# ReZero on one core: another cut of the load plan, with a multiply as the mark for the first store

## The chip, the cores and the metric

The kernel runs on one core of one Trainium2 chip. The metric is the device time of one execution in microseconds (us), the median of several runs. Before the change three runs gave 151.32, 151.74 and 152.62 us, so the time to beat is 151.74 us.

## The reference

Two arrays of bfloat16, `x` and `fx`, each of 512 x 32 x 640 elements, and one number `alpha`:

```
def reference(x, fx, alpha):
    return x + alpha * fx
```

Each array holds 20.97 MB. Both are read once and the output is written once, 62.92 MB in all, and the arithmetic on an element is one multiply and one add.

## The kernel before, in words

Each array is laid over the 128 partitions of the on-chip memory. A partition gets 81920 consecutive elements, which the kernel counts as 160 units of K = 512 elements (lines 12 and 13). One unit is 1 KiB on each partition, 128 KiB over all of them. Everything lives in one tile `t` of 160 + 47.5 units per partition (line 78): `x` has its place at units 0 to 160, is added to in place and stored from there. `fx` has no place of its own: it is put into units that `x` has not reached yet, or into the spare 47.5 units at the end.

The order of the work is written out by hand in `PLAN` (lines 27 to 56). The loop at lines 125 to 131 issues the steps in that order. A step's letter names its kind:

- `x a b` loads units a to b of `x` to their own place (line 98); `f a b p` loads units a to b of `fx` to place p (line 102). Both are issued on the queue of SyncE (SP).
- `a` loads `alpha` (line 106), spreads it over the partitions with one TensorE matmul (line 110) and copies it to the on-chip memory (line 112).
- `m a b` multiplies units a to b of `fx` by `alpha` in place, on VectorE (line 115); `c a b` adds them to `x`, on VectorE (line 118).
- `s a b` stores units a to b (line 121), on SP's queue too. Behind a bar stands a step that the store waits for although it needs none of its data ("begins late", line 131).

Waits for data and for places follow from overlapping ranges of `t`. A load that overwrites a place has to wait until the adds that read the old `fx` there are done. SP issues its steps strictly in order, so everything behind a waiting step waits as well; all loads and stores use one hardware queue that 16 DMA engines serve. VectorE takes its multiplies and adds in the order of the plan.

In the plan before, ten loads bring the data: `x` 0 to 8, 8 to 64, 64 to 96, 96 to 114, 114 to 155 and 155 to 160, and `fx` 0 to 64, 64 to 111.5, 111.5 to 137.5 and 137.5 to 160. The first five of them wait for nothing. `x` 96 to 114 overwrites `fx` 0 to 18, `x` 114 to 155 overwrites more of `fx` 18 to 64 (which lies at 96 to 160), and so on. The first store (units 0 to 64) is held back until the load of `fx` 137.5 to 160 has landed. The last load is `x` 155 to 160, with rows of 5 KiB. Three stores end the program: 0 to 64, 64 to 128 and 128 to 160. A last SP step (line 133) waits for all but the last store.

Of the kernel before, what the change touches and what calls it, by code (L numbers as in the profile page):

```python
# [1 line left out]

# [4 lines left out]

ALU = mybir.AluOpType
F32 = mybir.dt.float32

P = 128
K = 512
ROW = 160
SPARE = 47.5

LANES = 8

PLAN = """
x 0 8
a
x 8 64  # L30
f 0 64 96
x 64 96
f 64 111.5 160
m 0 18
c 0 18
x 96 114
m 18 64
c 18 64
x 114 155
m 64 88  # L40
c 64 88
f 111.5 137.5 158
m 88 111.5
c 88 111.5
f 137.5 160 184
m 111.5 113.5
c 111.5 113.5
x 155 160
s 0 64 | f 137.5 160 184
m 113.5 137.5  # L50
c 113.5 137.5
m 137.5 160
c 137.5 160
s 64 128
s 128 160
"""


@with_exitstack
def kernel(  # L60
    ctx: ExitStack,
    tc: tile.TileContext,
    x: bass.AP,
    fx: bass.AP,
    alpha: bass.AP,
    out: bass.AP,
):
    nc = tc.nc
    xv, fv, ov = (
        t.flatten_outer_dims().rearrange("(p n) d -> p (n d)", p=P) for t in (x, fx, out)  # L70
    )
    assert xv.shape[1] == ROW * K

    consts = ctx.enter_context(tc.tile_pool(name="consts", bufs=1))
    psum = ctx.enter_context(tc.tile_pool(name="psum", bufs=1, space=bass.MemoryType.PSUM))
    flat = ctx.enter_context(tc.tile_pool(name="flat", bufs=1))
    ctx.enter_context(tc.manual_schedule())
    t = flat.tile([P, int((ROW + SPARE) * K)], x.dtype, name="t")
    info = mybir.DependencyInfo(mybir.DependencyClass.Sync, mybir.DependencyReason.DATA)

    lanes = {}
    lies = []
    done = []

    def at(a, b):
        return t[:, int(a * K) : int(b * K)]

    def of(v, a, b):
        return v[:, int(a * K) : int(b * K)]

    def place(a, b):
        for c, d, p in reversed(lies):
            if c <= a and b <= d:
                return at(p + a - c, p + b - c)
        raise ValueError(f"fx {a} to {b} lies nowhere in one piece")

    def load_x(a, b):
        done.append(nc.sync.dma_start(out=at(a, b), in_=of(xv, a, b)))  # L98

    def load_f(a, b, p):  # L100
        lies.append((a, b, p))
        done.append(nc.sync.dma_start(out=at(p, p + b - a), in_=of(fv, a, b)))

    def load_alpha():
        a_n = consts.tile([LANES, 1], alpha.dtype, name="a_n")
        done.append(nc.sync.dma_start(out=a_n[:], in_=alpha[None, :].to_broadcast([LANES, 1])))  # L106
        ones = consts.tile([1, P], alpha.dtype, name="ones")
        nc.vector.memset(ones[:], 1.0)  # L108
        a_ps = psum.tile([P, 1], F32, name="a_ps")
        done.append(nc.tensor.matmul(a_ps[:], ones[:], a_n[0:1, :], start=True, stop=True))  # L110
        lanes["a"] = consts.tile([P, 1], F32, name="a_f")
        nc.vector.tensor_copy(out=lanes["a"][:], in_=a_ps[:])  # L112

    def multiply(a, b):
        done.append(nc.vector.tensor_scalar_mul(place(a, b), place(a, b), lanes["a"][:]))  # L115

    def add(a, b):
        done.append(nc.vector.tensor_add(at(a, b), at(a, b), place(a, b)))  # L118

    def store(a, b):  # L120
        done.append(nc.sync.dma_start(out=of(ov, a, b), in_=at(a, b)))

    does = {"x": load_x, "f": load_f, "a": load_alpha, "m": multiply, "c": add, "s": store}
    begun = {}
    for step in filter(None, PLAN.split("\n")):
        step, *later = step.split(" | ")
        what, *numbers = step.split()
        does[what](*map(float, numbers))
        begun[step] = done[-1]
        for other in later:  # L130
            tc.add_manual_dep(done[-1].ins, begun[other].ins.name, info, reason="begins late")

    rest = nc.sync.nop(nofuse=True)
    for i in done[:-1]:
        tc.add_manual_dep(rest.ins, i.ins.name, info, reason="all but the last store")


# [1 line left out]
_INS = ['x', 'fx', 'alpha']  # L139
_OUTS = [((512, 32, 640), 'bfloat16')]  # L140


# [23 lines left out]
```

## Time and profile before

| What | Value |
|---|---|
| median of 3 runs | 151.74 us (151.32 to 152.62) |
| time of the profiled execution | 151.5 us |
| its span, first to last instruction | 149.7 us |
| VectorE busy | 66.5 us, 44% |
| share of the 16 DMA engines' time | 97.9% |
| bytes moved | 62.92 MB, mean 420 GB/s |

The profiled execution took 151.5 us while its span is 149.7 us, so 1.8 us lie around the span. In the profile's rows DVE is VectorE, SPq is the sequencer that issues DMAs from SyncE, and a line such as L115 is a line of the kernel above. A DMA's time "to landing" counts from its issue until its last data has been confirmed, so it includes the time that it stands in the queue behind others. In the windows of the trace, a DMA packet (one row of a transfer) is counted whole where it begins, so the share of a short window can be far over 1.

### The profile page before, as it was taken

The page shows a single profiled execution, that of the slowest core. Times are in us where ns is not written, and L with a number is a line of the kernel's source. Part 1 is how long each engine was busy: PE and PEld are TensorE (multiplying, and loading weights), DVE is VectorE, ACT ScalarE, POOL GpSimd, SP SyncE. Part 2 cuts the span into 40 slices and gives each one's busy share as a digit, 9 for nine tenths or more (in the row PEclk, how much of TensorE's full clock was granted, in tenths as well). Part 3 has the DMA queues.
Part 4 walks back from the last instruction along what each step waited for, and adds up shares of the span by engine and source line. Part 5 has one row for each costly group of instructions (what it writes and reads, how often), then busy time and mean ns, then how long its engine had stood idle before and what let it go on. Part 6 is the DMA issues. An engine that isn't in the chain of part 4 may idle for free.

```text
span 149.7 us, 91 instructions
## 1 busy us (share of the span) xinstructions
PE 0.2 (0%) x1; PEld 0.1 (0%) x1; DVE 66.5 (44%) x16; POOL 0.2 (0%) x4
## 2 busy tenths in 40 slices
PE   0000000000000000000000000000000000000000
PEld 0000000000000000000000000000000000000000
DVE  0000000000079999999999944999990000000000
POOL 0000000000000000000000000000000000000000
DMA  5997996969999899979898989996997969696996
GB/s 173 598 429 306 490 525 280 560 280 560 403 429 420 357 520 494 429 323 500 359 527 370 427 377 414 456 480 280 560 508 333 560 280 560 280 560 280 420 420 280
DMA packets 1888, 62.92 MB, mean 420 GB/s; under 512 B 224, under 2 KB 224, under 8 KB 352
## 3 DMA queue, kind: packets, MB, share of 16 engines
q1 hardware_dynamic: 1888, 62.92, 97.9%
HBM read 41.94 MB, written 20.97 MB: 420 GB/s over the span
## 4 chain that ended last, share of the span: by engine, by line
DMA 36%; DVE 34%; issue 4%; SPq 1%; DVEq 0%
DMA t<-in_fx_dram 36%; DVE t L118 21%; DVE t L115 13%; SPq L98 0%; SPq L106 0%; DVEq L115 0%
## 5 line engine op out<-in xcount | busy, mean ns | idle before, releaser
L118 DVE TENSOR_TENSOR t<-t 128x12288 bf16<-128x12288 bf16 (+5 forms) x7 | 43.8, 6255 | 0.2
L115 DVE TENSOR_SCALAR t<-t,a_f 128x12288 bf16<-128x12288 bf16 (+5 forms) x7 | 22.8, 3264 | 40.0 <-DMA t<-in_fx_dram 40.0
L112 DVE COPY a_f<-a_ps 128x1 f32<-128x1 f32 x1 | 0.2, 158 | 4.6 <-PE a_ps L110 4.6
L108 DVE MEMSET ones<- 1x128 bf16 x1 | 0.2, 165 | 0.8 <-PEq L150 0.8
L110 PE MATMUL a_ps<-a_n,ones 1*128 1x1 bf16 x1 | 0.2, 158 | 5.4 <-DMA a_n<-in_alpha_dram 5.4
L150 POOL MEMSET const-uint8-127<- 128x1 uint8 x1 | 0.1, 102 | 0.0
L150 POOL MEMSET const-bfloat16-1.0<- 128x1 bf16 x1 | 0.1, 101 | 0.0
L110 PEld LDWEIGHTS <-ones 1*128 1x128 bf16 x1 | 0.1, 98 | 1.0 <-DVE ones L108 1.0
L150 POOL MEMSET const-float32-0.0<- 128x1 f32 x1 | 0.1, 98 | 0.2 <-issue 0.2
L150 POOL MEMSET const-float32-1.0<- 128x1 f32 x1 | 0.1, 98 | 0.0
## 6 DMA issues: line engine op xcount, KB each, us to landing
t<-in_x_dram SPq DMA_DIRECT2D x1, 7168.0 KB, 20.9
t<-in_fx_dram SPq DMA_DIRECT2D x1, 6080.0 KB, 63.0
t<-in_x_dram SPq DMA_DIRECT2D x1, 5248.0 KB, 15.6
t<-in_x_dram SPq DMA_DIRECT2D x1, 4096.0 KB, 49.1
out_dram<-t SPq DMA_DIRECT2D x1, 4096.0 KB, 36.7
t<-in_fx_dram SPq DMA_DIRECT2D x1, 3328.0 KB, 13.5
t<-in_fx_dram SPq DMA_DIRECT2D x1, 2880.0 KB
t<-in_x_dram SPq DMA_DIRECT2D x1, 2304.0 KB, 21.9
```

Source lines behind the costliest of these rows:

```text
L108: nc.vector.memset(ones[:], 1.0)
L110: done.append(nc.tensor.matmul(a_ps[:], ones[:], a_n[0:1, :], start=True, stop=True))
L112: nc.vector.tensor_copy(out=lanes["a"][:], in_=a_ps[:])
L115: done.append(nc.vector.tensor_scalar_mul(place(a, b), place(a, b), lanes["a"][:]))
L118: done.append(nc.vector.tensor_add(at(a, b), at(a, b), place(a, b)))
L150: nc = _bacc.Bacc("TRN2", target_bir_lowering=False, num_devices=1)
```

## The change

Only `PLAN` changes; the functions that carry out its steps stay as they are.

```diff
-x 0 8
+f 0 8 95
 a
-x 8 64
-f 0 64 96
-x 64 96
-f 64 111.5 160
-m 0 18
-c 0 18
-x 96 114
-m 18 64
-c 18 64
-x 114 155
-m 64 88
-c 64 88
-f 111.5 137.5 158
-m 88 111.5
-c 88 111.5
-f 137.5 160 184
-m 111.5 113.5
-c 111.5 113.5
-x 155 160
-s 0 64 | f 137.5 160 184
-m 113.5 137.5
-c 113.5 137.5
-m 137.5 160
-c 137.5 160
+f 8 65 103
+x 0 64
+x 64 95
+f 65 112.5 160
+m 0 8
+m 8 65
+c 0 8
+c 8 64
+c 64 65
+x 95 160
+m 65 95
+c 65 95
+f 112.5 142.5 160
+m 95 112.5
+c 95 112.5
+f 142.5 160 190
+m 112.5 134.5
+s 0 64 | m 112.5 134.5
+m 134.5 142.5
+c 112.5 142.5
+m 142.5 160
+c 142.5 160
 s 64 128
 s 128 160
```

There are eight loads in place of ten. `fx` comes first: units 0 to 8 and 8 to 65, laid at 95 to 160. Then come `x` 0 to 64 and 64 to 95 and `fx` 65 to 112.5, again five loads that wait for nothing. `x` 95 to 160 is one load with rows of 65 KiB; it waits for the add of unit 64 to 65. `fx` 112.5 to 142.5 is laid at 160 and waits for the add of 65 to 95; `fx` 142.5 to 160, the last load, is laid at 190 and waits for the add of 95 to 112.5. VectorE has 7 multiplies and 7 adds as before, in other pieces: the first two multiplies both stand ahead of the first add. The first store is held back until the multiply of 112.5 to 134.5 is done, and no longer by a load. The stores are the same three.

## The prediction

> **What bounds the kernel now.** I read the page first: its span, the busy engines and the DMA queue.
>
> ```profile
> span 149.7 us, 91 instructions
> PE 0.2 (0%) x1; PEld 0.1 (0%) x1; DVE 66.5 (44%) x16; POOL 0.2 (0%) x4
> DMA  5997996969999899979898989996997969696996
> q1 hardware_dynamic: 1888, 62.92, 97.9%
> ```
>
> The one queue fills 97.9% of the 16 DMA engines' time, VectorE 44% of its own. The change moves the same bytes, so only the queue's losses can be won: its start, its end, a gap, or a stretch that runs below its pace. To find them I followed the queue from landing to landing, with the SP rows of the timeline (issue), the issue table (time to landing), the chain (two waits for a load) and line 121 (the stores).
>
> ```profile
> 0.73 0.38 SPq L98 DMA_DIRECT2D t<-in_x_dram  x1
> 2.93 0.58 SPq L102 DMA_DIRECT2D t<-in_fx_dram  x1
> 49.59 19.05 SPq L98 DMA_DIRECT2D t<-in_x_dram  x2
> 68.31 0.33 SPq L98 DMA_DIRECT2D t<-in_x_dram  x1
> 78.24 10.05 SPq L102 DMA_DIRECT2D t<-in_fx_dram  x2
> 87.96 0.33 SPq L102 DMA_DIRECT2D t<-in_fx_dram  x1
> 93.04 0.33 SPq L98 DMA_DIRECT2D t<-in_x_dram  x1
> 99.10 0.35 SPq L121 DMA_DIRECT2D out_dram<-t  x1
> ...
> t<-in_fx_dram SPq DMA_DIRECT2D x1, 6080.0 KB, 63.0
> t<-in_x_dram SPq DMA_DIRECT2D x1, 5248.0 KB, 15.6
> t<-in_x_dram SPq DMA_DIRECT2D x1, 2304.0 KB, 21.9
> t<-in_x_dram SPq DMA_DIRECT2D x1, 1024.0 KB, 4.9
> t<-in_x_dram SPq DMA_DIRECT2D x1, 640.0 KB, 7.6
> ...
> 1.96 39.89 DMA t<-in_fx_dram
> 78.24 13.53 DMA t<-in_fx_dram
> ...
> DMA to landing us min/median/max: 20.9/36.4/36.7
> ...
> SPq L121 <- DMA t<-in_fx_dram: 5.7, 1, 5.7
> ```
>
> Issue plus time to landing gives: x 0 to 8 at 0.73 + 4.9 = 5.6; fx 0 to 64 at 1.96 + 39.89 = 41.85; fx 64 to 111.5 at 2.93 + 63.0 = 65.9; x 96 to 114 at 49.59 + 21.9 = 71.5; x 114 to 155 at 68.31 + 15.6 = 83.9; fx 111.5 to 137.5 at 78.24 + 13.53 = 91.77; fx 137.5 to 160 at 99.1 (the store waits 5.7 for it and is issued at 99.10); x 155 to 160 at 93.04 + 7.6 = 100.6; the last store, issued last with the longest time (its row comes below), at 112.28 + 36.7 = 149.0.
>
> **Pace by stage, in us per unit (128 KiB).** Units 8 to 64 of x and 0 to 64 of fx: (41.85 - 5.6) / 120 = 0.302. The next 79.5 units: (65.9 - 41.85) / 79.5 = 0.303. Then 5.6 / 18 = 0.31, 12.4 / 41 = 0.302, 7.9 / 26 = 0.303. Then fx 137.5 to 160: (99.1 - 91.77) / 22.5 = 0.326. Then 1.5 / 5 = 0.30. The three stores: (149.0 - 100.6) / 160 = 0.302. So the queue never stands still at its slowest engine, and one load runs below the pace: fx 137.5 to 160 takes 7.33 where 22.5 x 0.302 = 6.80, a loss of 0.5. Everything else together is some 0.25 over the pace. The reader should keep this ceiling: 5.6 + 472 x 0.302 = 148.1 for the last landing, against 149.0. About 0.9 us, 0.6%, is all that a perfect queue could win.
>
> Before the first store I also looked at short windows, since a landing shows the slowest engine only.
>
> ```profile
> 99.00:99.25 0.25, 0.00 (x0) 0.00 (x0) 0.25 (x1) 0.00 (x0) 1.00 0.98 410
> 99.25:99.50 0.25, 0.00 (x0) 0.00 (x0) 0.25 (x1) 0.00 (x0) 1.00 0.85 348
> 99.50:99.75 0.25, 0.00 (x0) 0.00 (x0) 0.25 (x1) 0.00 (x0) 1.00 0.26 102
> 99.75:100.00 0.25, 0.00 (x0) 0.00 (x0) 0.25 (x1) 0.00 (x0) 1.00 3.94 1675
> 0.00:1.70 1.70, 0.00 (x0) 0.10 (x1) 0.17 (x1) 0.20 (x4) 1.00 0.00 0
> ```
>
> The last columns are the DMA share and GB/s. The share sinks to 0.85 and 0.26 while the loads run out, and the store's first rows begin only after 99.75, some 0.65 to 0.9 behind its issue at 99.10. The first load of the program, issued at 0.73, begins no row before 1.70 either. So a transfer needs about 0.7 to 1.0 from issue to its first row, and the store was issued too late for the quick engines: they idle about 0.15 x 0.25 + 0.74 x 0.25 + 0.2 = 0.4 on the mean. The slowest engine is not among them, as the pace above shows: there the slow load hides the late store.
>
> **The change part by part.** The base is the profiled execution: span 149.7, time 151.5, so 1.8 around the span; the median of the runs shown is 151.74, 0.24 above it.
>
> First, *ten loads become eight.* What a load costs beside its bytes is read from the shortest one: x 155 to 160 landed 1.5 after its forerunner and its 5 units are 5 x 0.302 = 1.51 by the pace. With the rounding of the rows that is 0 to 0.1 a load, so two fewer give 0 to -0.2; I take -0.1. The Trainium skill, page "DMA: Bandwidth & Descriptors", section "Anatomy of one DMA", states a fixed cost of about 2.0 us for a DMA (fitted for the path issued from GpSimd); by that, paid in series, the two loads would be worth 4 us; the trace disagrees for a queue that is fed ahead, by the 1.5 of the shortest load.
>
> Second, *the order of loads.* Up to fx 65 to 112.5 the queue carries 8 + 57 + 64 + 31 + 47.5 = 207.5 units without a wait, as before (8 + 56 + 64 + 32 + 47.5). Cost nothing; alpha is again second in the queue. Later loads must be issued about 1.0 before the queue runs dry. For that I need VectorE's durations.
>
> ```profile
> L118 DVE TENSOR_TENSOR t<-t 128x23552 bf16<-128x23552 bf16 x1 | 12.4, 12426 | 0.0
> L118 DVE TENSOR_TENSOR t<-t 128x9216 bf16<-128x9216 bf16 x1 | 5.0, 4959 | 0.0
> L115 DVE TENSOR_SCALAR t<-t,a_f 128x23552 bf16<-128x23552 bf16 x1 | 6.3, 6349 | 0.0
> L115 DVE TENSOR_SCALAR t<-t,a_f 128x9216 bf16<-128x9216 bf16 x1 | 2.6, 2620 | 36.2 <-DMA t<-in_fx_dram 36.2
> 112.28 0.33 SPq L121 DMA_DIRECT2D out_dram<-t  x1
> ```
>
> From the two adds: (12426 - 4959) / 14336 = 0.521 ns an element, 0.267 us a unit, and 0.16 fixed. From the two multiplies: 0.260 ns, 0.133 us a unit, and 0.22 fixed. Now the new plan in time.
>
> - fx 0 to 8 lands at 5.6, fx 8 to 65 at 5.6 + 57 x 0.302 = 22.8; both multiplies are done by 22.8 + 7.8 = 30.6, under cover of the load of x 0 to 64, which lands at 42.2. Adds: 0 to 8 takes 2.3, 8 to 64 takes 15.1, 64 to 65 takes 0.43 (x 64 to 95 landed at 51.6), all done at 60.0. Then x 95 to 160 is issued. The queue holds fx 65 to 112.5 until that lands at 65.9: margin 5.9, less 1.0.
> - m 65 to 95: 4.2 from 65.9, to 70.1. c 65 to 95: 8.2, to 78.3. fx 112.5 to 142.5 is issued there; the queue holds x 95 to 160 until 65.9 + 65 x 0.302 = 85.5. Margin 7.2.
> - m 95 to 112.5 (2.6) runs meanwhile; c 95 to 112.5 waits for x until 85.5 and takes 4.8, to 90.4. fx 142.5 to 160 is issued there; the queue holds fx 112.5 to 142.5 until 94.6. Margin 4.2, less 1.0: the tightest of the three.
>
> SP waits in order, but behind each wait stand only later loads and stores that cannot go earlier. So the three waits cost nothing; if the cover of the last were gone, say VectorE 4 us late there, the queue would stand still for about 0.8.
>
> Third, *the row of 65 KiB.* The longest row in this trace is 64 KiB, so its price is not shown. If the row is moved in two pieces, 128 rows more, it costs what a load of the same 128 rows costs beside its bytes, 0 to 0.1. From below nothing is gained but those two loads already counted, since 64 KiB rows run at the common pace. From above: if a row is cut into 65 pieces of 1 KiB, there are 64 x 128 rows more; at 0 to 0.1 for 128 rows that is at most 6.4, and 3.2 at the middle. I take 0.05, nearest to the rows of 64 KiB. The Trainium skill, same page, section "Why a DMA increments its semaphore by 16 and not by 1", says that a contiguous row over 64 KiB is cut into equal pieces by software, and one without a fitting divisor falls into one piece per element; 33280 elements have the divisor 16640, so by that page two pieces; no run here shows it yet.
>
> Fourth, *no short last rows.* The last two loads, 22.5 and 5 units, took 7.33 + 1.5 = 8.83 where the pace gives 8.31. Of the new last loads one has 30 units, nearest to the 26 that ran at 0.303, and one 17.5 units, nearest to the 18 that ran at 0.31 (loss 0.1 to 0.15). Bounds: the loss of 0.5 vanishes, or it comes again in the new last load, since nothing in the trace says why it was slow. I take -0.4.
>
> Fifth, *the store's mark.* fx 112.5 to 142.5 lands at 94.6; m 112.5 to 134.5 takes 22 x 0.133 + 0.22 = 3.15, so the store is issued at about 97.8 and can begin its rows at 98.5 to 98.8. The last load lands at 94.6 + 17.5 x 0.302 + 0.1 = 100.0; its rows end earlier, on the quick engines at about 99.0 to 99.2 (before, they thinned out from 99.25 with the last landing at 100.6). So no engine waits for the store; 0.4 of mean idle goes. By itself that moves the end by 0, since the slowest engine did not wait; with the slow load gone, the store issued at 99.10 would have become the next limit and eaten up to half of the 0.4 of step four. Both go together; I count the store's mark as 0 to -0.2 beyond step four, and take -0.05. What is late next is nothing but the queue itself.
>
> The stores 64 to 128 and 128 to 160 are issued after c 112.5 to 142.5 (97.8 + 1.3 + 8.2 = 107.3) and c 142.5 to 160 (107.3 + 2.6 + 4.8 = 114.7), the last some 2.4 later than the 112.28 of before. The queue holds the first store until about 119: hidden.
>
> Sum: -0.1 + 0.05 - 0.4 - 0.05 = -0.5. Span 149.2, profiled time 151.0, against the median 151.74 - 0.5 = 151.24, so 151.2.
>
> **The rivals.**
>
> A, the forecast: no new wait, the queue at its pace, 151.2; with its bounds (losses of 0 to 0.9 in all) 150.8 to 151.7.
>
> B, the change wins nothing: the slow load was an accident of memory traffic and hits the new last load as well. For it speaks that no wait explains it (it was issued at 87.96, 3.8 before its forerunner landed); against it, that all other stages ran at 0.30 to 0.31. Then 151.7.
>
> C, the other side: the row of 65 KiB is cut fine and the load of x 95 to 160 itself becomes slow. Its landing carries everything behind it along: c 95 to 112.5, the last load, the stores. Price 3.2 (the middle above), so 151.24 + 3.2 = 154.4; it decides (slower by over 1%, 1.5 us) from about 2 us extra, an additional 0.03 us per unit. For it: no row over 64 KiB stands in this trace. Against it: rows of 5 to 64 KiB all run within 0.01 of the same pace but for the one load.
>
> D, each load pays its fixed cost in full, as in the page's rule above. Then two fewer would give 4 us, 147.7. The mechanism here would be a queue that drains between loads; the short load's 1.5 speaks against it almost alone.
>
> E, the last load is issued too late, because x 95 to 160 is one piece and its add begins only when all of it has landed. With 3.2 of net margin it needs a VectorE add of 8 in place of 4.8; then 0.1 to 1 us, up to 152.2.
>
> **How the numbers follow.** A difference of 1% (1.5 us) is about what a measurement of this kernel can tell from no change; the three runs before lie 1.3 apart. Chances: A 0.62, B 0.12, C 0.10, D 0.02, E 0.04, and 0.10 for what I do not see. Of A, 0.02 could fall below 150.2, since the ceiling of 0.9 and the spread of the runs together reach that far; of the unseen I give 0.04 to faster and 0.05 to slower by over 1%. Faster: 0.02 + 0.02 + 0.04 = 0.08. Slower: C's 0.10 + 0.05 = 0.15. The rest, 0.77, is within 1%. The range: from A's lower bound less the runs' spread below their median (150.8 - 0.4 = 150.4) to E's 152.2 plus as much, 152.6; it leaves out C, D and the far ends.
>
> **What would show it.** Right: the store's issue at 97.5 to 98.2; no window around 99 with a DMA share under 0.9 for half a us; x 95 to 160 landing at 85.2 to 86; SP's waits for VectorE ending at about 60, 78 and 90; the last landing at 148.3 to 148.7. Wrong: more packets than 8 x 128 + 3 x 128 + 128 rows and alpha's few would show a finely cut row (and a landing of x 95 to 160 past 87); a window without DMA at 65, 85 or 94 would show a late issue; fx 142.5 to 160 taking over 5.7 would show that the slow last load stays.

## The result and the profile after

The changed kernel takes 151.09 us, the median of 18 runs (150.95 to 151.29), against 151.75 us for the kernel before (18 runs, 151.32 to 152.62). The ratio is 0.9952 with a 95% interval of 0.9939 to 0.9965: a small gain of about half a per cent, within the 1% that the forecast counts as no change, and 0.1 us below the 151.2 that it named. The spread of the runs shrank as well, from 1.30 to 0.34 us.

The first lines of the changed kernel's page, then its issue table, the SP rows of its timeline and the pieces of its chain that end in a landing:

```profile
span 149.3 us, 84 instructions
PE 0.2 (0%) x1; PEld 0.1 (0%) x1; DVE 66.5 (45%) x16; POOL 0.2 (0%) x4
DMA  5969998969699999999999999899896969697993
DMA packets 1728, 62.92 MB, mean 421 GB/s; under 512 B 192, under 2 KB 192, under 8 KB 192
q1 hardware_dynamic: 1728, 62.92, 98.0%
...
t<-in_x_dram SPq DMA_DIRECT2D x1, 8320.0 KB, 25.8
t<-in_fx_dram SPq DMA_DIRECT2D x1, 7296.0 KB, 21.4
t<-in_fx_dram SPq DMA_DIRECT2D x1, 6080.0 KB, 63.0
out_dram<-t SPq DMA_DIRECT2D x1, 4096.0 KB, 33.7
t<-in_fx_dram SPq DMA_DIRECT2D x1, 2240.0 KB, 9.5
...
1.59 0.35 SPq L100 DMA_DIRECT2D t<-in_fx_dram  x1
3.09 0.51 SPq L100 DMA_DIRECT2D t<-in_fx_dram  x1
60.07 0.38 SPq L96 DMA_DIRECT2D t<-in_x_dram  x1
78.58 12.53 SPq L100 DMA_DIRECT2D t<-in_fx_dram  x2
98.15 17.05 SPq L119 DMA_DIRECT2D out_dram<-t  x3
...
1.98 40.34 DMA t<-in_x_dram
78.58 16.36 DMA t<-in_fx_dram
```

The profiled execution took 151.11 us, the span is 149.3. The landings, worked out as in the forecast: fx 8 to 65 at 1.59 + 21.4 = 23.0, x 0 to 64 at 42.32, fx 65 to 112.5 at 3.09 + 63.0 = 66.1, x 95 to 160 at 60.07 + 25.8 = 85.9, fx 112.5 to 142.5 at 94.94, and fx 142.5 to 160, issued at 78.58 + 12.53 - 0.33 = 90.8, at 100.3. (The 0.33 is the time of one issue; the row holds two.) So the last load took 5.4 for its 17.5 units, 0.306 a unit: no load runs clearly below the pace any more. The last store was issued at 98.15 + 17.05 - 0.35 = 114.9 and landed 33.7 later, at 148.6, where it was 149.0 before.

The windows around the first store, with the DMA share in the last but one column:

```profile
98.00:99.00 1.00, 0.00 (x0) 0.00 (x0) 1.00 (x2) 0.00 (x0) 1.00 1.17 502
99.00:99.25 0.25, 0.00 (x0) 0.00 (x0) 0.25 (x1) 0.00 (x0) 1.00 0.67 287
99.25:99.50 0.25, 0.00 (x0) 0.00 (x0) 0.21 (x2) 0.00 (x0) 1.00 2.44 1049
99.50:99.75 0.25, 0.00 (x0) 0.00 (x0) 0.25 (x1) 0.00 (x0) 1.00 5.47 2359
99.75:100.00 0.25, 0.00 (x0) 0.00 (x0) 0.25 (x1) 0.00 (x0) 1.00 1.82 786
100.00:100.25 0.25, 0.00 (x0) 0.00 (x0) 0.25 (x1) 0.00 (x0) 1.00 0.00 0
```

A row of 64 KiB occupies one of 16 engines for about 2.42 us, so one that begins in a window of 0.25 us adds 2.42 / 0.25 / 16 = 0.6 to its share. The reader can count engines: 2.44, 5.47 and 1.82 are 4, 9 and 3 engines that begin the store, each as its own loads run out, and by 100.0 all 16 have begun. Before the change there was a hole (0.26 in the window from 99.50), and one row more of the same view shows three engines that began after 100.25:

```profile
100.25:100.50 0.25, 0.00 (x0) 0.00 (x0) 0.25 (x1) 0.00 (x0) 1.00 1.82 786
```

### The profile page after: what moved, and what is told of

The parts are those of the page before. It is cut to its first block, busy times and chain, and to the rows that moved or that the text cites. A ratio compares the mean times of both kernels' runs of the same rounds, so it can differ in the third digit from the quotient of the medians.

```text
span 149.3 us, 84 instructions
## 1 busy us (share of the span) xinstructions
PE 0.2 (0%) x1; PEld 0.1 (0%) x1; DVE 66.5 (45%) x16; POOL 0.2 (0%) x4
## 2 busy tenths in 40 slices
DMA packets 1728, 62.92 MB, mean 421 GB/s; under 512 B 192, under 2 KB 192, under 8 KB 192
## 3 DMA queue, kind: packets, MB, share of 16 engines
q1 hardware_dynamic: 1728, 62.92, 98.0%
## 4 chain that ended last, share of the span: by engine, by line
DMA 38%; DVE 33%; another core or an unknown queue 4%; SPq 1%; issue 0%; DVEq 0%
DMA t<-in_x_dram 27%; DVE t L116 26%; DMA t<-in_fx_dram 11%; DVE t L113 7%; SPq L100 0%; SPq L104 0%; DVEq L116 0%
## 5 line engine op out<-in xcount | busy, mean ns | idle before, releaser
L116 DVE TENSOR_TENSOR t<-t 128x15360 bf16<-128x15360 bf16 (+4 forms) x7 | 43.6, 6252 | 16.6 <-DMA t<-in_x_dram 16.5
L113 DVE TENSOR_SCALAR t<-t,a_f 128x4096 bf16<-128x4096 bf16 (+4 forms) x7 | 22.8, 3265 | 25.7 <-DMA t<-in_fx_dram 25.7
## 6 DMA issues: line engine op xcount, KB each, us to landing
t<-in_x_dram SPq DMA_DIRECT2D x1, 8320.0 KB, 25.8
t<-in_fx_dram SPq DMA_DIRECT2D x1, 7296.0 KB, 21.4
out_dram<-t SPq DMA_DIRECT2D x1, 4096.0 KB, 33.7
```

## The experiments

The theory under test, T, follows the forecast: the queue's pace is fixed, and before the change two things at the join of loads and stores hid each other, a store issued too late for the quick engines and a few slow rows that held other engines back. Its rivals are that one part of the change alone did it: the mark, the longer last rows, the fewer loads, or the order.

The mark is the step that the first store waits for. Each ratio is taken against the kernel before as it ran beside that experiment (medians 151.71 to 151.83). Differences in us are taken from the 151.09 of the changed kernel, which was not run again beside them. "Packet records" are the trace's own list of rows, each with its start, its time and its size.

**The earlier mark alone, in the plan before.**

```diff
-s 0 64 | f 137.5 160 184
 m 113.5 137.5
+s 0 64 | m 113.5 137.5
 c 113.5 137.5
```

> The plan before, with one edit: the first store is released by the multiply of 113.5 to 137.5 (which ended at 96.3 in its profile) and no longer by the landing of fx 137.5 to 160 (99.1). Theory T (the forecast's): store mark and slow load hide each other, and the end is set by the slowest DMA engine; the mark alone wins 0 to 0.2 us, so 151.55 to 151.75 us, ratio 0.999 to 1.000, with no window of low DMA share around 99.5. Rival R (the late store is the whole loss of the plan before): 151.1 us, ratio 0.9955, as the changed kernel.

Measured: 152.13 us, ratio to the kernel before 1.0032 (1.0015 to 1.005). Both were wrong, by 0.4 and 1 us. The store was issued at 96.53, and the last load (x 155 to 160, issued at 93.20, 8.0 to landing) landed at 101.2 in place of 100.6. An early store did harm. The rows of this run's issues and of its last load:

```profile
93.20 0.33 SPq L98 DMA_DIRECT2D t<-in_x_dram  x1
96.53 0.35 SPq L121 DMA_DIRECT2D out_dram<-t  x1
...
t<-in_x_dram SPq DMA_DIRECT2D x1, 640.0 KB, 8.0
```

The runs without a mark and with a mark at 96, below, take this up.

**The mark a little later, in the changed plan.**

```diff
-s 0 64 | m 112.5 134.5
 m 134.5 142.5
+s 0 64 | m 134.5 142.5
```

> The changed plan, with the first store released by the next multiply, 134.5 to 142.5, which ended at 99.33, 1.2 us later than the mark of the changed kernel (98.15). Theory T: the store's rows then begin at about 100.2 to 100.4, while the slowest engine's loads end at 99.84; all engines wait, and the end moves by 0.4 to 0.5 us: 151.5 to 151.6 us. Rival (the mark matters nothing, the loads set the end): 151.1 us.

Measured: 151.63 us (151.53 to 151.74), ratio 0.9991 (0.9982 to 1.0001). Windows of this run, then its SP row:

```profile
99.00:99.25 0.25, 0.00 (x0) 0.00 (x0) 0.23 (x1) 0.00 (x0) 1.00 0.34 143
99.25:99.50 0.25, 0.00 (x0) 0.00 (x0) 0.24 (x1) 0.00 (x0) 1.00 0.02 0
99.50:99.75 0.25, 0.00 (x0) 0.00 (x0) 0.25 (x1) 0.00 (x0) 1.00 0.02 0
99.75:100.00 0.25, 0.00 (x0) 0.00 (x0) 0.25 (x1) 0.00 (x0) 1.00 0.00 0
100.00:100.25 0.25, 0.00 (x0) 0.00 (x0) 0.25 (x1) 0.00 (x0) 1.00 9.84 4194
...
99.25 0.35 SPq L119 DMA_DIRECT2D out_dram<-t  x1
```

The store is issued 1.1 us later than in the changed kernel. The loads have run out, and all 16 engines (9.84 / 0.6) begin the store in the same quarter of a microsecond after 100.0: 0.75 to 1.0 from issue to first row. T foretold 151.5 to 151.6; the rival, that the mark matters nothing, falls. And one thing more can be read: with everything else of the change in place but a late mark, the interval of the ratio includes 1. The rest of the change without the new mark wins nothing that can be told. (The store goes out 0.15 later here than the 99.10 of the plan before, so this is a little harsher than the old mark.)

**The earlier mark in the plan before, placed better.**

```diff
-s 0 64 | f 137.5 160 184
 m 113.5 137.5
-c 113.5 137.5
+c 113.5 119
+s 0 64 | c 113.5 119
+c 119 137.5
```

> The plan before, with the first store released at about 98.0 (the landing gave 99.1, the earlier trial 96.5): the add of 113.5 to 137.5 is cut at 119, and its first part is the mark. Theory T (late store and slow load hide each other, and a store issued far ahead slows the loads): the late store is cured, no load is slowed by it, and the slow rows at the start of fx 137.5 to 160 stay: 151.4 to 151.65 us. Rival R (the late store alone is the loss): 151.1 to 151.2 us. Rival S (the plan before cannot take an earlier store at all): 152.1 us, as with the mark at 96.5.

Measured: 151.66 us (151.16 to 152.83), ratio 0.9992 (0.9963 to 1.0022). The store went out at 98.55. Its windows:

```profile
99.25:99.50 0.25, 0.00 (x0) 0.00 (x0) 0.25 (x1) 0.00 (x0) 1.00 0.89 369
99.50:99.75 0.25, 0.00 (x0) 0.00 (x0) 0.25 (x1) 0.00 (x0) 1.00 5.37 2302
99.75:100.00 0.25, 0.00 (x0) 0.00 (x0) 0.25 (x1) 0.00 (x0) 1.00 2.77 1192
100.00:100.25 0.25, 0.00 (x0) 0.00 (x0) 0.25 (x1) 0.00 (x0) 1.00 0.24 102
100.25:100.50 0.25, 0.00 (x0) 0.00 (x0) 0.25 (x1) 0.00 (x0) 1.00 1.87 807
100.50:100.75 0.25, 0.00 (x0) 0.00 (x0) 0.25 (x1) 0.00 (x0) 1.00 0.61 262
```

The hole is gone (0.89, then 5.37), yet four engines (1.87 and 0.61) begin the store 0.5 to 1.0 us after the others, and each engine has the same 160 units of stores before it, so they end later by as much. T foretold 151.4 to 151.65, and the trace fits it: the slow engines of the old plan do not wait for the store, so an earlier store does not help them. The rivals fall, the full gain (151.1 to 151.2) by a little only: the interval reaches down to 0.9963, a gain of 0.56 us, so the times alone don't rule out that this mark wins something.

**Is it the short last rows?** The changed plan with the old kind of end:

```diff
-f 142.5 160 190
+f 142.5 155 190
+f 155 160 202.5
...
-m 142.5 160
-c 142.5 160
+m 142.5 155
+m 155 160
+c 142.5 155
+c 155 160
```

> The changed plan, with its last load (fx 142.5 to 160) cut in two, 142.5 to 155 and 155 to 160, so that the last rows are 5 KiB short as before the change; the last multiply and add are cut at 155 too. Theory T: one load more and short rows cost their fixed part alone, 0.05 us (0 to 0.1): 151.1 to 151.2 us. Rival (short last rows are what slowed the end of the loads): 0.4 us more, 151.5 us.

Measured: 151.10 us (150.99 to 151.65), ratio 0.9970 (0.9956 to 0.9983). Short last rows and a ninth load cost nothing that can be told from the 151.09 of the changed kernel. Whatever was slow in the old plan, rows of 5 KiB at the end were not it.

**What does a load cost beside its bytes?**

```diff
-x 0 64
+x 0 8
+x 8 16
...
+x 56 64
```

> The changed plan, with x 0 to 64 cut in eight loads of 8 units, seven loads more and 8 KiB rows. It measures the price of a load beside its bytes. By the rows of the changed kernel's trace (8 rows of 8 KiB at 309 ns an engine against one eighth of 8 rows of 64 KiB at 2418 ns) a load costs 0.06 us: 0.4 to 0.5 us for seven, 151.5 to 151.6 us; bounds of the forecast 0 to 0.7. Rival (each load pays about 2 us): 14 us, 165 us.

Measured: 151.57 us, ratio 0.9989 (0.9975 to 1.0003), with the DMA share of the page at 98.2%. Seven loads more cost 0.48 us against the changed kernel's median, 0.07 each. The price of 2 us a load falls.

**Is the order of the arrays of any account?**

```diff
-f 0 8 95
+x 0 8
 a
-f 8 65 103
-x 0 64
+x 8 64
+f 0 65 95
```

> The changed plan, with x first again: x 0 to 8, alpha, x 8 to 64, then fx 0 to 65 in one load, and from x 64 to 95 on as changed; still eight loads. Theory T: the first multiplies lose the load of x 0 to 64 that covered them; multiplies (9.1 us) and adds (17.8 us) start together at the landing of fx 0 to 65 at 42.3, so x 95 to 160 is issued at 69.3, its rows begin at about 70.2, while the queue runs dry at 65.1 to 65.7: a gap of 4.6 to 5.1 us, 155.7 to 156.2 us, ratio 1.026 to 1.030. Rival (the order of the arrays is of no account, the transfer is hidden anyway): 151.1 us.

Measured: 156.58 us, ratio 1.0324 (1.0306 to 1.0342). Windows of this run and the issue of x 95 to 160:

```profile
66.00:70.00 4.00, 0.00 (x0) 0.00 (x0) 4.00 (x3) 0.00 (x0) 1.00 0.00 0
70.00:71.00 1.00, 0.00 (x0) 0.00 (x0) 1.00 (x1) 0.00 (x0) 1.00 1.90 499
...
68.97 0.38 SPq L96 DMA_DIRECT2D t<-in_x_dram  x1
```

VectorE works through the first four microseconds shown while no row begins. The multiplies have lost the load that covered them, x 95 to 160 is issued at 68.97 in place of 60.07, and the queue stands dry. The gap measured 5.5 us against the changed kernel's median, a little over the 4.6 to 5.1 expected: by the packet records the queue ran dry at about 65.3 and began again at 70.0, and the fifteen rows that begin first after the gap took 1.7 to 2.3 us each, where the other rows of their size took 1.23. So the new order gives the cover that the load of 65 units in one piece needs. Whether the order wins anything by itself was not tried.

**No mark at all, a mark at 96, and no mark with small rows.** First the changed plan with a plain store:

```diff
-s 0 64 | m 112.5 134.5
+s 0 64
```

> The changed plan without the mark: the first store waits for its data alone and is issued right behind the last load, at about 91.1. Theory T: the queue works in order, the store's rows stand behind the last load's, and nothing changes: 151.0 to 151.1 us. Rival (an early store's writes mix with the loads and slow the last ones): the landing of fx 142.5 to 160 moves past 101, 151.3 us or more.

Measured: 151.69 us (151.53 to 153.30), ratio 1.0011 (0.9987 to 1.0035): 0.6 worse than the changed kernel. T, which foretold 151.0 to 151.1, was wrong here, and the rival came true in both its signs. SP rows and the last load of this run:

```profile
90.65 0.33 SPq L100 DMA_DIRECT2D t<-in_fx_dram  x1
91.07 0.39 SPq L119 DMA_DIRECT2D out_dram<-t  x1
t<-in_fx_dram SPq DMA_DIRECT2D x1, 2240.0 KB, 10.6
```

The load of fx 142.5 to 160, issued at the same time, takes 10.6 in place of 9.5: it lands at 101.25, not 100.3. The packet records show where: of the 49 rows of this load that begin after 97.2, 30 took over 0.73 us, up to 1.49, where its rows take 0.67. In the changed kernel's trace no row of it that begins after 94.2 did. Next a mark between:

```diff
-m 112.5 134.5
-s 0 64 | m 112.5 134.5
+m 112.5 122.5
+s 0 64 | m 112.5 122.5
+m 122.5 134.5
```

> The changed plan, with the multiply that is the mark cut at 122.5, so that the first store is issued at about 96.6 in place of 98.15. Theory T (a store that stands behind the last load early slows its last rows): between no mark (151.69 us) and the changed kernel (151.09 us), 151.3 to 151.5 us, with rows of fx 142.5 to 160 over 0.7 us long after 97.2. Rival (only the very early issue at 91 harms): 151.1 us.

Measured: 151.60 us (151.06 to 152.13), ratio 0.9968 (0.9944 to 0.9993), with the store issued at 96.34 and 10.3 for the last load. The traced execution has the slow rows again, though fewer and later: ten that begin from 98.3 on took 0.72 to 1.13 us. The median lies a little above the expected 151.3 to 151.5, but three of the twelve runs took 151.06 to 151.18, and the interval overlaps that of the changed kernel (0.9939 to 0.9965). So the harm is seen in the trace, and its size is not settled. Last, the store cut small, without a mark:

```diff
-s 0 64 | m 112.5 134.5
+s 0 8
+s 8 64
```

> The changed plan without a mark, as in the run that gave 151.69 us, but with the first store cut in two, 0 to 8 and 8 to 64, so that the rows that stand behind the last load are 8 KiB and not 64 KiB. If the engines begin a fixed number of rows ahead to read what they will write, small rows take less from the loads: 151.2 to 151.4 us. If they read a fixed number of bytes ahead, or if the mere presence of a store slows loads: 151.7 us (0.06 us for the additional store included).

Measured: 151.75 us (151.47 to 153.12), ratio 0.9998 (0.9969 to 1.0028), with 10.2 for the last load. Smaller rows behind the load do not spare it, so the idea of a fixed number of rows read ahead finds no support here. Whether it is bytes read ahead or the mere presence of the store stays open. The Trainium skill, page "DMA: Bandwidth & Descriptors", section "Two DMAs through the same engine are not ordered", says that the descriptors of a queue start in order but are pipelined, with separate queues for reads and writes; that leaves room for a store's reads beside a load's writes, and no run here shows them directly.

**The size of the first load.** One first load of 65 units, and one of 2:

```diff
-f 0 8 95
+f 0 65 95
 a
-f 8 65 103
```

> The changed plan with fx 0 to 65 as one first load, alpha behind it: seven loads. Theory T: alpha lands at about 23, the first multiplies end at about 34, still ahead of x 0 to 64 at 42.2; one load less wins 0.05 us: 151.0 to 151.1 us. Rival (the small first load pays for itself, by a quicker start of the queue or by alpha's early arrival): 151.3 us or more.

Measured: 151.53 us, ratio 0.9986 (0.9975 to 0.9997), 0.44 worse than the changed kernel.

```diff
-f 0 8 95
+f 0 2 95
 a
-f 8 65 103
+f 2 65 97
...
-m 0 8
-m 8 65
-c 0 8
-c 8 64
+m 0 2
+m 2 65
+c 0 2
+c 2 64
```

> The changed plan, with a first load of 2 units (rows of 2 KiB) in place of 8: fx 0 to 2, alpha, fx 2 to 65; the first multiply and add are cut at 2. With one first load of 65 units the slowest engine was 0.42 us later after unit 65 than in the changed kernel. Theory T (the loss at the start grows with the size of the first rows): 0.1 to 0.15 us less than the changed kernel, 150.95 to 151.0 us. Rival (the first load must be long enough to cover the next load's start and alpha's): 151.2 to 151.5 us.

Measured: 153.24 us, ratio 1.009 (1.006 to 1.0121), 2.15 worse. The load that ends at unit 65, first in the run with seven loads (issued at 0.73), then in the run with 2 units (issued at 1.58):

```profile
t<-in_fx_dram SPq DMA_DIRECT2D x1, 8320.0 KB, 22.7
```

```profile
t<-in_fx_dram SPq DMA_DIRECT2D x1, 8064.0 KB, 23.6
```

It lands at 23.4 and 25.2; in the changed kernel at 23.0. So the 0.44 of the first run is lost before unit 65, and most of the loss of the second. In both, T was wrong: neither the longer nor the shorter first load is better than 8 units. The rival came true with 65 units. With 2 units it was right in kind, but the loss is larger than it had it.

The packet records of the run with 2 units say more. (Its traced execution took 154.23, 1.0 above the median.) The 2 KiB rows are over by 3.1, and fourteen engines have begun the next load by 3.43, but two begin it only at 3.87 and 4.63. The first row of the later one takes 3.56 us, where the rows of this load take 2.38. These two pass unit 65 at 23.8 and 24.8, the others by 23.1, and two engines still work on loads until 102.4 and 103.0, when the others are done by 100.4. A late alpha isn't the reason: its copy on VectorE ran at 3.76, in the changed kernel at 6.16. Why two engines began so late, and why the first rows are slow, stays open.

**The kernel before, a second trace.**

> The kernel before once more, for a second trace of its end. If the slow load of fx 137.5 to 160 belongs to the plan, it takes 7.2 to 7.5 us from the landing of its forerunner again and the time is 151.4 to 151.8; if it is an accident of memory traffic, it is near 6.8 to 7.0 in this trace, or another load is slow.

Measured: 151.53 us, one run. From the forerunner's landing at 91.8 (the 13.5 of its issue table, behind an issue at 78.33) to the store's issue at 99.15, which the landing of fx 137.5 to 160 releases, that load took 7.3 again where the pace gives 6.8.

```profile
78.33 10.05 SPq L102 DMA_DIRECT2D t<-in_fx_dram  x2
99.15 13.56 SPq L121 DMA_DIRECT2D out_dram<-t  x3
...
t<-in_fx_dram SPq DMA_DIRECT2D x1, 3328.0 KB, 13.5
```

The packet records of all four traces of the old plan (two as it was, two with an earlier mark) agree: four to six rows of fx 137.5 to 160 that begin between 90.7 and 91.7 took 0.91 to 1.75 us, where its rows take 0.86. So the slow start belongs to the plan before and is no accident of one execution. It has not wholly gone in the changed plan: there two rows at the start of the last load took 1.16 and 0.98 in place of 0.67, but they did not make their engines the last. What makes these rows slow stays open.

No experiment's median lies below that of the changed kernel.

## Why the prediction was right, point by point

The signs that the forecast named for being right came: the store's issue at 98.15 (97.5 to 98.2 foretold), x 95 to 160 landed at 85.9 (85.2 to 86), the loads that wait for VectorE were issued at 60.07, 78.58 and 90.8 (60, 78 and 90), the DMA share near 99 was below 0.9 for a quarter of a us only, and the last landing was at 148.6 (148.3 to 148.7).

- *The bound.* The queue stayed full and at its pace: x 95 to 160 took 85.9 - 66.1 = 19.8 for 65 units, 0.304 each, the stores (148.6 - 100.3) / 160 = 0.302. Two readings of the plan before were a little off: the stages beside the slow load add up to 0.33 over the pace, not 0.25 (149.0 - 148.1 - 0.53), and the engines idled 0.32 on the mean before the first store by the packet records, not 0.4. In the changed kernel they idle 0.00 there. The forecast's landings (42.2, 65.9, 85.5, 94.6, 100.0) came within 0.4 us (42.32, 66.1, 85.9, 94.94, 100.3), and its issues (60.0, 78.3, 90.4, 97.8) too.
- *Two fewer loads, -0.1.* Right within its bounds: seven loads cost 0.48, so two would be worth 0.14. The one load more of the run with short last rows cost nothing that could be told.
- *The row of 65 KiB, +0.05.* Right in kind: there are 1728 packets, of which 192 are under 512 bytes. The other 1536 are 12 x 128: 8 loads, 3 stores and one more set of 128, so each row went in two pieces. The Trainium skill (page "DMA: Bandwidth & Descriptors", section "Why a DMA increments its semaphore by 16 and not by 1") speaks only of what comes of such a row if software cuts it into equal pieces. That it was cut so here is shown by the packets. Rival C had no ground.
- *The order, 0, with cover.* The cover is real: without it the run with x first lost 5.5 us. The 0 itself was not measured.
- *No short last rows, -0.4.* The size fits, the name of the step does not. With the short rows put back, the time is the same. What went is most of the slow start of a load of the old plan, and the forecast had noted that nothing in the trace says why it was slow. Nothing here says it either. So this term, the largest of the sum, came true partly by luck: the forecast had no reason why the slow load should go, and gave 0.12 to its staying.
- *The store's mark, -0.05.* This is the term that was mis-sized. The forecast saw that the slow load hides the late store and that with the slow load gone a store at 99.10 would eat up to 0.2 of the gain. In the changed plan a mark 1.1 us later (99.25) costs 0.54, nearly the whole gain, and the intervals of the ratios don't touch (0.9982 to 1.0001 against 0.9939 to 0.9965). In the old plan an earlier store gives 0.9992. So neither cure alone wins anything that can be told, and both together win 0.66 us: the forecast's half a microsecond is a joint gain, which it split as if the parts added up. By the times alone this is not clear of noise, since the interval of the 0.9992 is wide (0.9963 to 1.0022). The traces, below, carry it.
- *A store ahead of need, priced at nothing.* The forecast counted only a store that comes too late. Against the store at 98.15, the one issued at 91.07 lost 0.60 and the one at 99.25 lost 0.54. The one at 96.34 lost 0.51 by the medians, but its interval overlaps. So the new mark sits in a narrow place, a narrower one than the forecast knew.

One relation in the packet records ties the traces together. The last row of all ends 48.3 us after the last of the 16 engines begins the first store; with the late mark it is 48.5:

| Run | last engine begins the store | last row ends |
|---|---|---|
| before | 100.27 | 148.61 |
| earlier mark (96.53) in the old plan | 100.86 | 149.17 |
| earlier mark (98.55) in the old plan | 100.54 | 148.85 |
| changed | 99.84 | 148.16 |
| late mark | 100.24 | 148.77 |
| no mark | 100.84 | 149.15 |
| mark at 96 | 100.57 | 148.89 |
| first load of 2 units | 103.05 | 151.36 |

So in these traces everything that the plans differ by has happened when the last engine turns to the store. That engine can be late because its own loads were slow (the old plan, no mark, the first load of 2 units) or because the store was not there yet (the late mark, where all 16 wait, 0.68 on the mean). The changed kernel has neither, and that is the gain. Why its loads start with fewer slow rows is the open end.

The spread of the runs fits this. The kernel with the late mark has its runs close together (151.53 to 151.74): the late store lines up all engines. Those of the old plan, with an early store or with the first load of 2 units scatter over 1.1 to 1.8 us, as would be if their end is that of whichever engine was held back. With one trace to each run this is not shown.

## What to carry to other kernels

In this kernel one queue is the bound and 16 engines each work off their own share, and the end was that of the slowest engine: a gap that the others had before it was worth little until the slow engine was cured. So test two cures together before either is dropped. And look for the best moment to release a transfer of the other direction. Of the moments tried here, the best lay 1.2 us before the loads' rows ran out on the quickest engine (98.15 against 99.35), a little over the 0.75 to 1.0 from an issue to its first row. Both a later and a much earlier store lost.

## What the runs showed of the hardware that was not expected

- A store that waits in the same queue behind a load slows that load's last rows: the landing of the last load went from 9.5 to between 10.2 and 10.6 us after its issue when the store was issued 2 to 7 us earlier, and rows that take 0.67 took up to 1.49.
- The first load has a best size among those tried: 2 units cost 2.15 us and 65 units 0.44 us more than 8.
- A queue that has run dry costs more than the gap: 5.5 us where it stood still for 4.7. The first rows of a load behind the gap are slow (1.7 to 2.3 us in place of 1.23). So are the fourteen rows that begin first in the changed kernel's trace (0.69 to 1.44 in place of 0.31).
